# PSUM banks by step in the opening of a fused linear-attention and mixture-of-experts kernel, and norms in two halves

## The chip, the cores and the metric

One core of one Trainium2 chip. The metric is the device time of one execution in microseconds (us). A profile is one traced execution; its span is some 1.7 to 2.2 us shorter than the reported time of the same execution, so spans are compared with spans and times with times.

## The reference

Linear attention (no softmax over positions) feeds four dense experts whose outputs are added with normalised weights (condensed):

```python
def phi(x): return np.where(x > 0, x, np.exp(x) - 1.0) + 1.0
q_p, k_p = phi(q), phi(k)                       # 8 batches, 8 heads, 576 positions, 64 per head
kv  = np.einsum('bhsd,bhse->bhde', k_p, v)
num = np.einsum('bhsd,bhde->bhse', q_p, kv)
den = np.einsum('bhsd,bhd->bhs', q_p, np.sum(k_p, axis=2))[..., None] + 1e-06
x   = num / den                                 # -> 4608 rows of 512
p   = domain_probs / (domain_probs.sum(-1, keepdims=True) + 1e-09)
for e in range(4):
    out += p[:, e:e+1] * (np.maximum(x @ w1[e], 0) @ w2[e])    # 512 -> 1024 -> 512
```

## The kernel before

The kernel has an opening (0 to 27 us), in which batch 0 goes through attention as four *head pairs* while weights stream in; a first part (27 to 80 us), in which the experts run on batches 0 and 1 as plain matmuls; and the *unit* stage (80 us to the end), which is the bulk. The change touches the opening. There each pair takes these steps, on the engine named:

phi of k and q (ACT the exponential, DVE the rest); k-v sums (PE), copied out as `kvz` (ACT); transposed q (PE), copied as `qT` (ACT); products and denominators (PE); reciprocal and multiplication, the *norm* (DVE); transposed x (PE), copied (ACT). When all four pairs are there, the first layer of expert 0 can finish.

In PSUM the kernel keeps eight tiles of 512 columns, called banks here: `l1b[0..2]`, `l2b[0..3]` and `at`. A scheduler inside the kernel orders the operations, each with an engine, an estimated time, a priority and the keys it reads and writes; the framework then guards each PSUM tile as a whole (in the trace before, steps on disjoint columns of `l2b[2]` wait for each other, 5.1 us in six rows of the wait list). The part that decides who shares a bank:

```python
    def first_attention(pr, pri, step):
        ni = pr % 2
        num = (at, l2b[1])[ni]                                  # products
        kv3 = l2b[2][:, 0 : 2 * DE].rearrange(...)              # k-v sums        \
        d0 = 136 + ni * 2 * C
        den = l2b[2][:, d0 : d0 + 2 * C].rearrange(...)         # denominators     > one bank
        xt = l2b[2].bitcast(FP16)[:, NT : 2 * NT]               # transposed x    /
        # ...
        def nd(cs):
            for c in cs:                                        # two matmuls a chunk
                nc.tensor.matmul(out=num[:, c * P : (c + 1) * P], lhsT=qT[:, c],
                                 rhs=kvz[:, :, 0:D], start=True, stop=True)
                nc.tensor.matmul(out=den[:, c], lhsT=qT[:, c],
                                 rhs=kvz[:, :, D:DE], start=True, stop=True)
        # ...
        parts = 2 if pr == DC - 1 else 1                        # last pair in halves
        # ... one entry per step and half, for example:
            add("DVE", 0.93, pri + 5.5 * step, u, lambda cs=cs: norm(cs),
                r=(("num", ni), ("l2b2n", ni)), w=(("xk", pr),))
```

The leftover rows of batch 0 (64 positions beside the 512) are normalised in two groups through the bank `at` in the middle of the first part:

```python
    def rest_late(pri):
        # ...
        for p0, n in ((0, 3), (3, 1)):
            def mm(...):   nc.tensor.matmul(out=slot[pr - p0], ...)   # slot lies in `at`
            def norm(...): ...                                        # DVE, reads `at`
```

And where the scheduler expects PE to be idle early on, throw-away matmuls are put in, meant to keep its clock up ("fillers", `keep_warm()`). In the trace of the kernel before, fillers of 256 columns start 0.21 us apart until 7.6 us and, where they follow each other, 0.11 us apart after it; the granted clock is recorded there as 1.00 from 7.66 to 492.35 us.

Of the kernel before, what the change touches and what calls it, by code (L numbers as in the profile page):

```python
# [10 lines left out]
FP32 = mybir.dt.float32  # L11
FP16 = mybir.dt.float16
AO = mybir.AluOpType
AF = mybir.ActivationFunctionType
# [123 lines left out]
def kernel(  # L138
# [10 lines left out]
    nc = tc.nc  # L149

    B, H, S, D = q.shape
# [3 lines left out]
    P = 128  # L155
    NT = 512
    C = NT // P
    R = S - NT
    DE = D + 1
    DC = Dm // P  # L160
# [5 lines left out]
    WARM, COLD = 21.0, 28  # L166
# [3 lines left out]
    pl = Plan()  # L170
# [5 lines left out]
    def sb(name, shape, dt):  # L176
        return pc.tile(shape, dt, tag=name, name=name)
# [32 lines left out]
    x_b = [sb(f"x{i}", [P, C, Dm], FP16) for i in range(2)]  # L210
# [3 lines left out]
    identh = s15h[:, 0:P]  # L214
# [15 lines left out]
    v_o = [  # L230
        t[:, i * NT : (i + 1) * NT].rearrange("p (h c d) -> p h c d", h=2, c=C)
        for t in (X3[2], T3[0]) for i in range(2)
    ]
# [3 lines left out]
    v_r, kp_r = (  # L237
        T2[2][:, i * 2 * P : (i + 1) * 2 * P].rearrange("p (a b d) -> p a b d", a=2, b=2)
        for i in (2, 3)
    )  # L240
# [6 lines left out]
        A["t", 3, 1 + i] = [("kqp", 2 + i, 0), ("kqp", 2 + i, 1)]  # L247
        A["t", 2, i] = [("ek", 2 + i, 0), ("ek", 2 + i, 1)]
    A["t", 2, 2], A["w1x", 2, 0] = [("k_r", g) for g in range(DC)] + ["v_r", "kp_r"], ["ek_r"] + [("v_r32", g) for g in range(DC)]
    A["l2b1"], A["at"] = [("num", 1)], [("num", 0)]  # L250
    A["l2b3"] = [("tq", 0), ("tq", 1)]
    ones = sb("ones", [P, 2, 1], FP16)
    rc4 = sb("rc4", [P, 2, 2 * C], FP32)
    xt0 = s4_b[1].rearrange("p a c t -> p a (c t)")
    hts = [h_b[i][:, t, f].rearrange("p c t -> p (c t)") for i in range(2)
           for t in range(2) for f in range(2)]
# [16 lines left out]

    def lk(i):

        return ("l2b2k", ("l2b2n", 0), ("l2b2n", 1), "l2b2x") if i == 2 else ("l2b%d" % i,)

    def stage_keys(i):

# [196 lines left out]
    def first_attention(pr, pri, step):  # L476

        kq, sk = kqs[pr], stage_keys(pr)
        ek, kqp, vh, kvz, qT = ek_o[pr], kqp_o[pr], v_o[pr], kvs[pr], qT_b[pr % 2]
        fs = slice(pr * P, (pr + 1) * P)  # L480
        g = slice(pr * 2 * R // DC, (pr + 1) * 2 * R // DC)
        ni = pr % 2
        num = (at, l2b[1])[ni]
        tq = tbank[:, ni * NT : (ni + 1) * NT]
        kv3 = l2b[2][:, 0 : 2 * DE].rearrange("p (h e) -> p h e", h=2)
        d0 = 136 + ni * 2 * C
        den = l2b[2][:, d0 : d0 + 2 * C].rearrange("p (c h) -> p c h", h=2)
        xt = l2b[2].bitcast(FP16)[:, NT : 2 * NT]

        def phi(i, cs):  # L490
            o = kqp[:, i, cs].rearrange("p c h d -> p h c d")
            nc.vector.tensor_scalar(o, kq[:, i, :, cs], 0.0, 1.0, AO.max, AO.add)
            nc.vector.tensor_tensor(out=o, in0=ek[:, i, :, cs], in1=o, op=AO.min)

        def turn(cs):
            for c in cs:
                nc.tensor.transpose(
                    out=tq[:, c * P : (c + 1) * P], in_=kqp[:, 1, c], identity=identh
                )

        def kv():
            parts = [(kqp[:, 0, c], vh[:, :, c], ones) for c in range(C)]
            parts += [(kp_r[g, t], v_r[g, :, t], ones[g]) for t in range(2)]
            for i, (kk, vv, oo) in enumerate(parts):
                for o, x in ((kv3[:, :, 0:D], vv), (kv3[:, :, D:DE], oo)):
                    nc.tensor.matmul(out=o, lhsT=kk, rhs=x, start=(i == 0 and x is vv),  # L506
                                     stop=(i == len(parts) - 1), skip_group_check=True)

        def kvcopy():
            nc.scalar.copy(kvz[0:D, 0, :], kv3[0:D, 0, :])  # L510
            nc.scalar.copy(kvz[D:P, 1, :], kv3[D:P, 1, :])

        def nd(cs):
            for c in cs:
                nc.tensor.matmul(out=num[:, c * P : (c + 1) * P], lhsT=qT[:, c],
                                 rhs=kvz[:, :, 0:D], start=True, stop=True)
                nc.tensor.matmul(out=den[:, c], lhsT=qT[:, c],
                                 rhs=kvz[:, :, D:DE], start=True, stop=True)

        def norm(cs):  # L520
            rc = rc4[:, ni].rearrange("p (c h) -> p c h", h=2)[:, cs]
            nc.vector.reciprocal(rc, den[:, cs])
            nc.vector.tensor_tensor(  # L523
                out=x_b[0][:, cs, fs].rearrange("p c (h d) -> p c h d", h=2),
                in0=num.rearrange("p (c h d) -> p c h d", c=C, h=2)[:, cs],
                in1=rc[:, :, :, None].broadcast_to([P, cs.stop - cs.start, 2, D]),
                op=AO.mult,
            )

        def turn_x(cs):  # L530
            for c in cs:
                nc.tensor.transpose(  # L532
                    out=xt[:, c * P : (c + 1) * P], in_=x_b[0][:, c, fs], identity=identh
                )

        parts = 2 if pr == DC - 1 else 1
        m = C // parts
        halves = [(range(i * m, i * m + m), slice(i * m, i * m + m),
                   slice(i * m * P, (i * m + m) * P)) for i in range(parts)]

        def add(eng, dur, pri, u, fn, r, w):

            end = u == parts - 1
            r = tuple(r) if end else tuple((x, u) for x in r)
            w = tuple(w) if end else tuple(w) + tuple((x, u) for x in w)
            pl.add(eng, dur / parts + (0.1 if parts > 1 else 0), pri + 0.01 * u, fn, r=r, w=w)

        for i in range(2):
            pl.add("ACT", 0.62, pri + i * step, lambda i=i: nc.scalar.activation(
                ek[:, i], kq[:, i], AF.Exp), r=(sk[i],), w=(("ek", pr, i), (("ek", pr, i), 0)))  # L550
        pl.add("DVE", 0.9, pri + step, lambda: phi(0, slice(0, C)),
               r=(sk[0], ("ek", pr, 0)), w=(("kqp", pr, 0),))
        pl.add("PE", 0.5, pri + 4 * step, kv,
               r=(("kqp", pr, 0), ("v_o", pr), "v_r", "kp_r"), w=("l2b2k",))
        pl.add("ACT", 0.45, pri + 4.5 * step, kvcopy, r=("l2b2k",),
               w=(("kvz", pr), (("kvz", pr), 0)))
        for u, (cr, cs, ts) in enumerate(halves):
            add("DVE", 0.9, pri + 2 * step, u, lambda cs=cs: phi(1, cs),
                r=(("ek", pr, 1),), w=(("kqp", pr, 1),))
            add("PE", 0.24, pri + 3 * step, u, lambda cr=cr: turn(cr), r=(("kqp", pr, 1),),  # L560
                w=(("tq", ni),))
            add("ACT", 0.58, pri + 3.5 * step, u, lambda ts=ts: nc.scalar.copy(
                qT.rearrange("p c t -> p (c t)")[:, ts], tq[:, ts]), r=(("tq", ni),),
                w=(("qT", ni),))
            add("PE", 0.36, pri + 5 * step, u, lambda cr=cr: nd(cr),
                r=(("qT", ni), ("kvz", pr)), w=(("num", ni), ("l2b2n", ni)))
            add("DVE", 0.93, pri + 5.5 * step, u, lambda cs=cs: norm(cs),
                r=(("num", ni), ("l2b2n", ni)), w=(("xk", pr),))
            add("PE", 0.25, pri + 6 * step, u, lambda cr=cr: turn_x(cr), r=(("xk", pr),),
                w=("l2b2x",))  # L570
            add("ACT", 0.58, pri + 6.5 * step, u, lambda ts=ts: nc.scalar.copy(  # L571
                xt0[:, pr, ts], xt[:, ts]), r=("l2b2x",), w=(("s4", 1, pr),))

    def attention(b, pr, pe_mode, pri, step):

# [210 lines left out]
    def first_l1(e, pri, step, nb):  # L786
        ht = []
        banks = [(l1b[i], "l1b%d" % i) for i in range(3)]
        if nb > 3:
            banks[2:] = [(l2b[0], "l2b0"), (at, "at"), (l2b[3], "l2b3"), (l2b[1], "l2b1")]  # L790
            banks += [(l1b[2], "l1b2")]
        ht = [rot("ht", len(hts)) for _ in range(FC)]

# [375 lines left out]
                rest_maps(b, False, t - 2)  # L1169
            attention(b, pr, False, t, 1.5)  # L1170

    def keep_warm():

        nc.tensor.matmul(out=l1b[2][:, 256:512], lhsT=identh,  # L1174
                         rhs=qTr[0][:, 0:2].rearrange("p a t -> p (a t)"), start=True, stop=True)

    prep(0)
# [11 lines left out]
    with tc.manual_schedule(  # L1189
        engines={  # L1190
            mybir.EngineType.PE,
            mybir.EngineType.Activation,
            mybir.EngineType.DVE,
            mybir.EngineType.Pool,
            mybir.EngineType.SP,
        }
    ):
        todo = pl.order()
        free = 0.0
        warm = True  # L1200
        for o in todo:
            warm = warm and "l1b2" not in o["w"] and o["start"] < WARM
            if o["eng"] == "PE" and warm:
                gap = o["start"] - free
                for _ in range(int((gap - 0.25) / 0.115) - (COLD if free == 0.0 else 0)):
                    keep_warm()
                free = o["start"] + o["dur"]
            o["fn"]()

# [29 lines left out]
```

## Time and profile before

| before | |
|---|---|
| time, 3 runs | 497.99 us median (497.81 to 498.1) |
| profiled span | 495.8 us |
| x of batch 0 complete | 23.05 us |
| second layer of expert 0 starts | 26.60 us |
| first matmul of the unit stage | 79.66 us |

The prediction below shows the page, the waits and the timeline of the opening. In a timeline row the columns are: start (us from the start of the span), duration, engine, source line, operation, output and input names, shapes, count, and in brackets the idle time just ahead and what ended it. Matmul rows overlap at their ends (a row of 37.45 + 1.89 = 39.34, and the next from 39.18), so the pitch from one row's start to the next, divided by the count, is PE's rate.

```profile
37.45 1.89 PE L761 MATMUL l1b<-s,w 128*128 128x512 f16 x8
39.18 0.22 PE L453 MATMUL at<-s,qTr 128*128 128x130 f16 x1
```

```profile
38.41 0.55 DVE L461 TENSOR_TENSOR xr_sb<-at,rc 64x384 f16<-64x384 f32 x1
```

DVE is done with the first group in `at` at 38.96; PE writes the second group at 39.18, on its own pace (8 matmuls, 1.73 us), so 0.22 us of slack is left.

```profile
78.58 0.63 ACT L408 ACTIVATE ek<-kqr 64x512 f16<-64x512 f32 x1 [0.20 <-DMA kqr<-in_k_dram]
```

ACT waits here 0.20 us for the leftover rows of k of batch 2, and after this does copies that PE needs. A *product of the first unit* (no product of attention) is one row of eight matmuls of 128 columns on PE (L924). The first one starts at 79.66, and the third, in PE's timeline of the kernel before, at 80.93, which is 1.27 us later:

```profile
80.93 0.61 PE L924 MATMUL l1b<-xs,w1x 128*128 128x128 f16 x8
```

### The profile page before, as it was taken

The numbers are of one execution on the slowest core, as the hardware profiler recorded it, in microseconds if no ns is written. First come the engines' busy times: TensorE is split into PE (matmuls) and PEld (weight loads), VectorE is DVE, ScalarE is ACT, GpSimd is POOL, SyncE is SP. The second block draws the span as 40 slices with busy tenths as digits, with TensorE's granted clock in tenths as the row PEclk, the third lists the DMA queues.
The fourth block names the chain that finished last, engine by engine and source line by source line (L and its number), as shares of the span: only waits on it lengthen the run. The fifth ranks groups of instructions, "written<-read, shape, count | busy, mean of one in ns | idle before, by whom it ended". The sixth has DMA issues, their size and how long they took to land.

```text
span 495.8 us, 15025 instructions
## 1 busy us (share of the span) xinstructions
PE 485.8 (98%) x6108; PEld 430.3 (87%) x6108; DVE 411.5 (83%) x1041; ACT 365.2 (74%) x687; POOL 41.1 (8%) x66
## 2 busy tenths in 40 slices
PE   7899999999999999999999999999999999999995
PEld 6544557999999999999999999999999999999994
DVE  6598999999998989899988899899988676767664
ACT  5536679978977898769876997689766767676641
POOL 7656600000000000000000000000000000000000
PEclk9999999999999999999999999999999999999998
DMA  8999958956755765876556655755623333523211
GB/s 227 203 234 226 269 124 218 192 123 179 118 156 124 161 143 155 131 177 150 133 135 159 131 155 128 179 127 119 161 54 87 35 97 44 87 45 86 46 44 42
DMA packets 125541, 66.98 MB, mean 135 GB/s; under 512 B 94592, under 2 KB 119696, under 8 KB 125472
## 3 DMA queue, kind: packets, MB, share of 16 engines
q1 hardware_dynamic: 115808, 51.99, 47.5%
q0 software_dynamic: 9344, 13.71, 13.6%
q8 instruction: 47, 0.77, 0.7%
q10 hardware_dynamic: 320, 0.33, 0.2%
q14 instruction: 22, 0.18, 0.1%
HBM read 45.16 MB, written 9.44 MB: 110 GB/s over the span
## 4 chain that ended last, share of the span: by engine, by line
PE 97%; DVE 1%; ACT 1%; issue 0%; DVEq 0%
PE l1b L924 40%; PE l2b L1000 39%; PE l2b L772 6%; PE l1b L761 5%; PE at L664 2%; PE l1b L1174 2%; PE at L640 1%; PE l2b L506 0%; DVE ot L1064 0%; PE l2b L761 0%; ACT s L571 0%; PE at L643 0%; PE l2b L532 0%; DVE x L523 0%; PE l2b L616 0%
## 5 line engine op out<-in xcount | busy, mean ns | idle before, releaser
L924 PEld LDWEIGHTS <-w 128*128 128x128 f16 x2048 | 134.1, 98 | 5.4
L938 ACT ACTIVATE h<-l1b 128x512 f16<-128x512 f32 x128 | 76.6, 599 | 53.3 <-PE l1b L924 50.4
L1000 PE MATMUL l2b<-w,h 128*128 128x256 f16 x768 | 115.1, 273 | 0.0
L1000 PE MATMUL l2b<-t,s 128*128 128x256 f16 x768 | 114.6, 273 | 0.0
L924 PEld LDWEIGHTS <-w1x 128*128 128x128 f16 x1536 | 100.2, 98 | 3.8 <-issue 0.3
L1000 PEld LDWEIGHTS <-s 128*128 128x128 f16 x1024 | 90.2, 98 | 6.2
L944 DVE CUSTOM_DVE_ANT_0 h<-l1b,p 128x512 f16<-128x512 f32 x64 | 44.1, 689 | 44.0 <-PE l1b L924 41.2
L924 PE MATMUL l1b<-xT,w 128*128 128x128 f16 x1024 | 78.1, 219 | 0.0
L924 PE MATMUL l1b<-xs,w1x 128*128 128x128 f16 x1024 | 78.1, 219 | 0.0
L924 PE MATMUL l1b<-xs,w 128*128 128x128 f16 x1024 | 78.1, 219 | 0.0
L884 ACT ACTIVATE xp<-x,p_nat 128x512 f16<-128x512 f16 x112 | 77.3, 721 | 0.4
L1000 PEld LDWEIGHTS <-h 128*128 128x128 f16 x768 | 67.3, 98 | 4.5
L986 DVE TENSOR_TENSOR s<-h 128x512 f16<-128x512 f16 x128 | 53.8, 420 | 2.1
L941 ACT COPY l1b<-l1b 128x512 f32<-128x512 f32 x64 | 36.7, 574 | 12.3 <-PE l1b L924 11.7
L941 ACT COPY u<-l1b 128x512 f32<-128x512 f32 x64 | 37.4, 585 | 10.9 <-PE l1b L924 10.2
L944 DVE CUSTOM_DVE_ANT_0 h<-l1b,u 128x512 f16<-128x512 f32 x64 | 43.8, 684 | 1.7 <-PE l1b L924 0.6
L941 ACT COPY p<-l1b 128x512 f32<-128x512 f32 x64 | 37.3, 583 | 8.6 <-PE l1b L924 7.4
L902 DVE TENSOR_TENSOR xs<-xT,xs 128x256 f16<-128x256 f16 x128 | 36.8, 288 | 3.8 <-DVE xs L902 0.5
L924 PE MATMUL l1b<-xT,w1x 128*128 128x128 f16 x512 | 39.0, 219 | 0.0
L1000 PE MATMUL l2b<-w,s 128*128 128x256 f16 x256 | 38.4, 273 | 0.0
L605 ACT ACTIVATE ek<-kq 128x512 f16<-128x512 f32 x54 | 33.7, 628 | 0.1
L986 DVE TENSOR_TENSOR s<-s,h 128x512 f16<-128x512 f16 x64 | 27.2, 424 | 5.6
(155 smaller groups left out, 580.7 us busy)
## 6 DMA issues: line engine op xcount, KB each, us to landing
w<-in_moe_w_dram POOLq DMA_DIRECT2D x32, 256.0 KB, 8.0
out_dram<-ot SPq DMA_DIRECT2D x16, 512.0 KB, 3.4
kq<-in_k_dram SPq DMA_DIRECT2D x26, 256.0 KB, 3.3
kq<-in_q_dram SPq DMA_DIRECT2D x26, 256.0 KB, 3.4
vs<-in_v_dram SPq DMA_DIRECT2D x24, 256.0 KB, 3.9
xT<-xp SPq DMA_TRANSPOSE x64, 3.1
kq<-in_k_dram POOLq DMA_DIRECT2D x3, 256.0 KB, 7.1
vs<-in_v_dram POOLq DMA_DIRECT2D x3, 256.0 KB, 7.1
```

The costliest lines, as they stand in the source:

```text
L605: pl.add("ACT", 0.55, pri + i * step, lambda i=i: nc.scalar.activation(ek[:, i], kq[:, i], AF.Exp), r=(sk[i],), w=(("ek", ei, i),))
L664: nc.tensor.matmul(out=slot[c - c0], lhsT=qT[:, c] if c < C else qTr[par][:, pr], rhs=kvz, start=True, stop=True,)
L761: nc.tensor.matmul(out=bank[:, ts], lhsT=w1_sb[e][:, dc, fj * P : (fj + 1) * P], rhs=xt0[:, dc, ts], start=(dc == 0), stop=(dc == DC - 1 a ...
L772: nc.tensor.matmul(out=bank, lhsT=hts[ht[fj]][:, c * P : (c + 1) * P], rhs=w2_sb[e][:, fj, :], start=(fj == 0), stop=(fj == FC - 1),)
L884: pl.add("ACT", 0.6, pri, lambda c=c, src=src, ps=ps: nc.scalar.activation(xp[:, c, :], src, AF.Copy, scale=ps), r=r, w=(("xp", xi, c),))
L902: lambda o=o, a=a, b_=b_: tt(out=o, in0=a, in1=b_, op=AO.subtract),
L924: nc.tensor.matmul(out=bank[:, fc * P : (fc + 1) * P], lhsT=wt[:, kc, fc * P : (fc + 1) * P], rhs=r[:, kc, :], start=(start and fc == 0 an ...
L938: return lambda: nc.scalar.activation(o, bank, AF.Relu)
L941: return lambda: nc.scalar.copy(o, bank)
L944: return lambda: nc.vector._custom_dve(TENSOR_ADD_SAT, out=o, in0=bank, in1=t, s0=BIG, s1=0.0)
L986: pl.add("DVE", 0.36, U(n + 1) + d - 0.5, lambda i=i, a=a, b_=b_, alu=alu: tt(out=s4[:, i], in0=a, in1=b_, op=alu), r=r, w=(Q(i),))
L1000: nc.tensor.matmul(out=l2b[bank][:, half * HD : (half + 1) * HD], lhsT=a[:, c, :], rhs=w[:, c], start=(opens and first and c == 0), stop=( ...
```

## The change

The intent: no step of a head pair should wait for another step merely because both are in one PSUM bank. k-v sums keep `l2b[2]` alone; products and denominators go into one bank together, two chunks in `at`, two in `l2b[1]`; transposed x goes to `l1b[2]` (its last half to `l2b[3]`, by then free). Four chunks with their denominators would be 4 x 130 = 520 columns, and each of the kernel's PSUM tiles has 512, so if products and denominators are to share one, they have to be split in two: in this plan the banks and the halves come together. In return products and denominators become one matmul per chunk, and all pairs are normalised in halves, not only the last. The banks of the first layer are dealt again, and fillers get another bank.

```diff
-        num = (at, l2b[1])[ni]
-        tq = tbank[:, ni * NT : (ni + 1) * NT]
+        nds = [bank[:, 0 : C * DE].rearrange("p (c h e) -> p c h e", c=2, h=2)
+               for bank in (at, l2b[1])]
         kv3 = l2b[2][:, 0 : 2 * DE].rearrange("p (h e) -> p h e", h=2)
-        d0 = 136 + ni * 2 * C
-        den = l2b[2][:, d0 : d0 + 2 * C].rearrange("p (c h) -> p c h", h=2)
-        xt = l2b[2].bitcast(FP16)[:, NT : 2 * NT]
+        tq = tbank[:, 0:NT]
+        last = pr == DC - 1
+        xts = [l1b[2].bitcast(FP16), tbank if last else l1b[2].bitcast(FP16)]
 ...
-        def nd(cs):
-            for c in cs:
-                nc.tensor.matmul(out=num[:, c * P : (c + 1) * P], lhsT=qT[:, c],
-                                 rhs=kvz[:, :, 0:D], start=True, stop=True)
-                nc.tensor.matmul(out=den[:, c], lhsT=qT[:, c],
-                                 rhs=kvz[:, :, D:DE], start=True, stop=True)
+        def nd(u):
+            for c in range(2):
+                nc.tensor.matmul(out=nds[u][:, c], lhsT=qT[:, 2 * u + c], rhs=kvz,
+                                 start=True, stop=True)
 ...
+        for u in range(2):
+            pl.add("PE", 0.12, pri + (5 + 0.1 * u) * step, lambda u=u: nd(u),
+                   r=(("qT", ni), ("kvz", pr)), w=(("at", "l2b1")[u],))
+            pl.add("DVE", 0.63, pri + (5.5 + 0.1 * u) * step, lambda u=u: norm(u),
+                   r=(("at", "l2b1")[u],), w=(("xk", pr, u),))
+        bk = ("l1b2", "l2b3" if last else "l1b2")
 ...
-            banks[2:] = [(l2b[0], "l2b0"), (at, "at"), (l2b[3], "l2b3"), (l2b[1], "l2b1")]
+            banks[2:] = [(l2b[0], "l2b0"), (l2b[2], "l2b2"), (at, "at"), (l2b[1], "l2b1")]
             banks += [(l1b[2], "l1b2")]
 ...
-    def keep_warm():
-        nc.tensor.matmul(out=l1b[2][:, 256:512], lhsT=identh, ...
+    def keep_warm(bank):
+        nc.tensor.matmul(out=bank[:, 256:512], lhsT=identh, ...
```

## The prediction

> **What bounds the kernel now.** I read the page first (busy shares, slices, the chain that ended last), then the waits of the first 30 us, then that stretch's timeline engine by engine, since the change touches the opening alone. The page:
>
> ```profile
> PE 485.8 (98%) x6108; PEld 430.3 (87%) x6108; DVE 411.5 (83%) x1041; ACT 365.2 (74%) x687; POOL 41.1 (8%) x66
> ...
> PE   7899999999999999999999999999999999999995
> ...
> PE 97%; DVE 1%; ACT 1%; issue 0%; DVEq 0%
> ```
>
> PE sets the end. In the timeline 8 matmuls of 128 columns take 0.45 us (56 ns each), 8 of 512 take 1.73 (216 ns): from 26.6 us to about 490 it streams with no listed idle. So time can be won only before 26.6 us, where PE waits or does filler ("l1b L1174", throw-away matmuls against a cold PE). One row per reader, what it waited for, total, count, longest, for 0 to 30 us:
>
> ```profile
> DVE rc L522 <- PE l2b L506: 1.7, 2, 0.9
> ...
> PE l2b L517 <- ACT s L571: 1.0, 2, 0.6
> ...
> ACT kvz L510 <- DVE rc L522: 0.8, 1, 0.8
> ...
> DVE rc L522 <- ACT s L571: 0.7, 1, 0.7
> ...
> ACT s L510 <- PE l2b L532: 0.6, 1, 0.6
> ...
> PE l2b L506 <- DVE rc L522: 0.3, 1, 0.3
> ```
>
> None of these rows is a data dependence. The reciprocal (L522) needs the denominators (L517), not the next pair's k-v products (L506); the denominators do not need the previous pair's copy of x (L571). All live in one bank, l2b[2]: kv sums, two pairs' denominators, transposed x. Sum 5.1 us, over three engines, so partly parallel. How the waits line up at the last pair (PE's timeline, then ACT's):
>
> ```profile
> 19.28 0.40 PE L532 MATMUL l2b<-s,x 128*128 128x128 f16 x4 [0.22 <-DVE x L523]
> ...
> 20.50 0.17 PE L517 MATMUL l2b<-s,qT 128*128 128x2 f16 x1 [0.60 <-ACT s L571]
> ...
> 22.91 0.70 PE L761 MATMUL l2b<-s,w 128*128 128x512 f16 x3
> ...
> 26.60 3.62 PE L772 MATMUL l2b<-w,h 128*128 128x512 f16 x16
> ```
>
> ```profile
> 19.86 0.59 ACT L571 COPY s<-l2b 128x512 f16<-128x512 f16 x1 [0.50 <-PE l2b L517]
> 21.95 0.37 ACT L571 COPY s<-l2b 128x256 f16<-128x256 f16 x1 [1.50 <-PE l2b L532]
> 22.68 0.37 ACT L571 COPY s<-l2b 128x256 f16<-128x256 f16 x1 [0.36 <-PE l2b L532]
> ```
>
> The last half of x lands at 22.68+0.37 = 23.05. Of the first layer of expert 0 (32 matmuls x 0.216 = 6.9 us) half is then still to do: 26.6-23.05 = 3.55 us. At 26.6 the second layer starts.
>
> Last, POOL's issues, which show when weights land. From the eighteenth load on, issue n seems to wait for transfer n-8: the issue at 26.30 waited for kqr, which had been issued exactly eight loads earlier. So the starts of the waiting issues date the landings:
>
> ```profile
> 19.84 1.06 POOL L292 DMA_DIRECT2D w<-in_moe_w_dram  x2 [0.75 <-DMA w<-in_moe_w_dram]
> ...
> 26.30 0.72 POOL L292 DMA_DIRECT2D w<-in_moe_w_dram  x1 [0.41 <-DMA kqr<-in_q_dram]
> ...
> 46.16 0.72 POOL L292 DMA_DIRECT2D xp<-in_k_dram  x1 [0.54 <-DMA w<-in_moe_w_dram]
> ```
>
> By this count the last quarter of expert 0's w1 lands at 19.8, its w2 at 21.1 to 25.1, expert 1's w1 by 30.7, expert 2's w1 at 46.1.
>
> [...]every wait above is between disjoint columns of one bank. [...] Here the first fillers take 5.26/24 = 219 ns, later ones 1.25/10 = 125; no gap after 8 us reaches 1 us[...].
>
> **The change, part by part.**
>
> Removed: the shared bank. kv keeps l2b[2] alone; products go with their denominators, two chunks each, into `at` and l2b[1]; transposed x goes to l1b[2], the last half to l2b[3]. PE also saves: 4 x (128-column + 2-column) at 0.08 us a couple = 0.34 us a pair become 4 matmuls of 130 columns at about 0.055 = 0.22 us; four pairs, 0.5 us.
>
> Added: norms in halves for all pairs. Measured half: reciprocal start 20.86 to next start 21.41 = 0.55 us; two = 1.1, against 0.24+0.61 = 0.85 for a whole one. Three pairs x 0.25 = 0.75 us of DVE, which idles over 5 us between 9 and 24. The last pair loses its halves in phi, transpose and qT: about 0.4+0.2+0.2 = 0.8 us of latency.
>
> Moved: first-layer banks. `at` and l2b[1] now stay taken until the last norm, l1b[2] until the last pair's first x copy; l2b[2] takes l2b[3]'s place.
>
> The new opening by hand, from measured durations, each step at the later of its data and its engine. Data are unchanged: they come by DMA, k of pair 3 about 13.0 (issued 7.87, 5.1 to landing), q 13.7 (8.58+5.1), v 14.9. Up to the second phi of pair 1 (ends 11.23) all is as before.
> DVE, the busiest engine here: norm 0 (products at 10.8 to 11.2, no longer behind pair 1's kv) 11.2 to 12.3; phi of pair 2, q (0.95 a phi) to 13.2; norm 1 13.4 to 14.5, its products waiting for qT (copied 12.4 to 13.0 after kvcopy); the two phi of pair 3 14.5 to 16.3; norm 2 16.3 to 17.4, its products long ready.
> Pair 3 on PE and ACT: transposes of q end 16.8 (0.41 after phi), qT 17.45 (0.59), first products 17.75; DVE norm 3 17.8 to 18.95 in halves; first half of x transposed 18.45 to 18.7 and copied 18.8 to 19.15; second half transposed by 19.3, copied by 19.7.
> So x is complete about 19.7 in the ideal order, say 20.5 in the real one, instead of 23.05.
>
> PE then: with four banks usable early, two quarters of the contraction (8 matmuls) fit before 18.6, when quarter three's weights (18.5) and x of pair 2 (about 18.5) are there. Left: 24 x 0.216 = 5.2 us and 0.2 of transposes, so the first layer ends at 24.0. This is PE-bound; x has some 1.5 us to spare. Before: 26.6 to 26.8. Ideal gain 2.7 us. I take off 0.5 for in-order holes (the old opening has such ones at 18.9, 19.9 and 21.4) and 0.2 for what follows downstream: **2.0 us**. After the opening PE's work is unchanged, so the end moves by the same amount: 498.0-2.0 = **496.0 us**.
>
> **Rivals.**
>
> *Weights take the place of the wait.* With L1 of expert 1 at 33.5-2.0 = 31.5 its weights (by 30.7) are there, with 0.8 us to spare; that of expert 2 starts at 48.8-2.0 = 46.8 against 46.1. DMA was over full share from 10 to 60 us, so loads cannot come earlier. It speaks for this that a gain over 2.7 us would touch the landing; against it, that a gain of 2 does not. If it binds: 496.5 to 497.
>
> *DVE becomes the bound.* DVE is nearly gapless from 62 to 92 us (18.9 of 20 us busy in 80 to 100) and sits at 91% in 100 to 200. Moving PE earlier moves its deadlines. But DVE's own start, the first relu at 23.76, moves too, and around 74 to 78 it does work due much later (weight sums of the last expert, phi of batch 2). If it binds, half the gain goes: 497.
>
> *The new banks bring new waits.* Three banks are locked later than before, and fillers now write l2b[2], where kvcopy reads, so a filler can hold PE until a copy is done. For it: the remainder after x is bigger, 3.5 to 4.3 us. Against: PE has work in other banks meanwhile. If the order came out badly: 498 to 499.
>
> *All goes to plan:* 495.2.
>
> **Range and chances.** The size of the shift is what I doubt, not its direction. 8 in 10: 495.1 to 497.4. 2% is 10 us, more than all idle PE time before 26.6; so faster by over 2% 0.01, within 2% 0.98, slower 0.01.
>
> **What would show each step.** Right: the six wait rows gone or under 0.3 us; the last x copy done at 20 to 21; the second layer starting at 24.2 to 25.2 without PE idle after it; the unit stage (first L924) at 77.2 to 78, not 79.7; the gap in the start of the second layer equal to the gap in the span. Wrong: PE waiting for a DMA or for DVE between 26 and 100 us; x late because norms queue on DVE; holes of PE over 0.5 us between 17 and 24; fillers waiting for ACT on l2b[2]; matmuls of twice the duration, a lost clock.

Some passages are cut, and the cuts marked. The forecast: 2.7 - 0.5 - 0.2 = 2.0 us. The DMA that it calls "over full share" has shares of 1.07 to 1.19 in the trace from 10 to 60 us, taken in stretches of 2 to 8 us; that loads could not come earlier for this reason is the author's estimate.

## The result

| | before | after |
|---|---|---|
| time, median (range), 4 runs each | 497.9 us (497.51 to 498.1) | 496.46 us (496.36 to 497.32) |
| ratio | | 0.9976 [0.9959, 0.9993] |
| profiled span | 495.8 us | 494.7 us |
| x of batch 0 complete | 23.05 | 20.69 |
| second layer of expert 0 starts | 26.60 | 24.67 |
| first matmul of the unit stage | 79.66 | 77.98 |
| fifth product of the first unit | 81.82 | 80.61 |
| from there to the end of the span | 414.0 | 414.1 |

Ratios here and below are the mean time of one kernel's runs over that of the kernel before in the same rounds, so not quite the ratio of the medians; the brackets are 95% intervals. Every run gave correct results. The change gains about 0.2%, well inside the 2% within which a time counts as the same.

The page of the kernel after, busy shares and the chain that ended last:

```profile
PE 484.2 (98%) x6092; PEld 429.3 (87%) x6092; DVE 413.0 (83%) x1045; ACT 364.8 (74%) x686; POOL 41.0 (8%) x66
...
PE 91%; DVE 3%; DMA 3%; ACT 1%; POOL 1%; issue 1%; DVEq 0%; SPq 0%; ACTq 0%
```

PE has 16 matmuls fewer (four pairs of four chunks, each with one matmul where there were two), DVE four operations more and 1.5 us more of work. The chain is the telling line: before it was PE to 97%, now DMA and DVE have 3% each.

The waits of all engines from 0 to 30 us, of the kernel after; columns: engine, what it was about to write, line, releaser, total, times, longest:

```profile
PEld L528 <- DVE x L519: 1.3, 3, 0.7
...
DVE rc L518 <- PE at L513: 1.1, 1, 1.1
...
PE at L513 <- ACT kvz L509: 0.9, 1, 0.9
```

The six false waits of before (5.1 us) are gone. What is left follows the data: x is transposed after its norm, the reciprocal waits for its own denominators, the products for `kvz`. PE's timeline of the kernel after shows what bounds the opening now:

```profile
14.48 0.22 PE L504 MATMUL l2b<-t 128*128 128x128 f16 x1 [0.59 <-DMA t<-in_v_dram]
...
19.25 0.38 PE L750 MATMUL l1b<-s,w 128*128 128x512 f16 x1 [0.45 <-ACT s L533]
...
23.59 1.25 PE L750 MATMUL l1b<-s,w 128*128 128x256 f16 x6
24.67 1.67 PE L761 MATMUL l2b<-w,h 128*128 128x512 f16 x7
```

First, PE waits at 14.48 for v of pair 2, which is a load: in the profiled executions of the kernels below that share this opening this start lies anywhere from 14.08 to 15.60 us. Second, from 19.25 PE runs without a listed wait to the second layer. The last copies of x, ACT of the kernel after:

```profile
19.77 0.37 ACT L533 COPY s<-l1b 128x256 f16<-128x256 f16 x1 [0.57 <-PE l1b L528]
20.32 0.37 ACT L533 COPY s<-l2b 128x256 f16<-128x256 f16 x1 [0.17 <-PE l2b L528]
```

x is complete at 20.32 + 0.37 = 20.69, four microseconds before the first layer ends.

So the opening gives 26.60 - 24.67 = 1.93 us, but the span only 1.1. From the fifth product of the first unit to the end both kernels take 414 us, so the 0.83 us are lost between 24.67 and 80.61. The same milestones, as differences, localise it: from the second layer of expert 0 to the first layer of expert 1 both take 6.90; from there to expert 1's second layer 7.46 before and 7.72 after (0.26 lost); from there to the first unit matmul 38.70 and 38.69; from there to the fifth product 2.16 and 2.63 (0.47 lost); and 0.11 over the remaining 414 us.

**First loss, at 37.5 us.** PE's timeline and then DVE's of the kernel after:

```profile
35.56 1.89 PE L750 MATMUL l1b<-s,w 128*128 128x512 f16 x8
37.51 0.22 PE L451 MATMUL at<-s,qTr 128*128 128x130 f16 x1
```

```profile
36.91 0.55 DVE L459 TENSOR_TENSOR xr_sb<-at,rc 64x384 f16<-64x384 f32 x1
```

The eight matmuls now take 1.95 us to the next row instead of 1.73, and the next row begins just after DVE has read `at` (36.91 + 0.55 = 37.46). No wait is listed, since gaps this short do not reach the list; the pitch shows it. PE had come 1.89 us earlier to this place (37.45 to 35.56), DVE only 1.50 (38.41 to 36.91), and the slack was 0.22: 1.89 - 1.50 - 0.22 = 0.17, near the 0.22 us that were lost in this pitch. DVE started 2.47 us earlier (its first relu at 21.29 instead of 23.76) and works back to back from there, but between this relu and the first scaling of the second layer's rows it does nine weight sums instead of eight, each 0.6 us. That is most of the 0.97 us by which it came less early to the norm.

**Second loss, at 79.7 us.** ACT's and then PE's timeline of the kernel after:

```profile
75.38 1.33 ACT L873 ACTIVATE xp<-x,p_nat 128x512 f16<-128x512 f16 x2
78.04 0.63 ACT L406 ACTIVATE ek<-kqr 64x512 f16<-64x512 f32 x1 [1.33 <-DMA kqr<-in_k_dram]
```

```profile
79.72 0.61 PE L913 MATMUL l1b<-xs,w1x 128*128 128x128 f16 x8 [0.20 <-ACT l1b L930]
```

The load of k's leftover rows, issued at 73.56, lands only at 78.04, 4.5 us later; before it took 3.3. ACT waits 1.33 us for it, the copy that PE needs next stands behind this exponential in ACT's order and is late, and PE waits: its third product starts 79.72 - 77.98 = 1.74 us after the first, instead of 1.27. This is the whole 0.47.

Why the load takes 1.2 us longer is the question that took most of the experiments. One more view, the DMA queues in half a microsecond: the kernel before from 73.0 to 73.5,

```profile
q8 instruction: 1, 0.02, 12.3%
```

and the kernel after from 75.0 to 75.5:

```profile
q1 hardware_dynamic: 170, 0.04, 37.1%
q8 instruction: 1, 0.02, 12.0%
```

(Columns: queue and kind, packets, MB, share of the 16 DMA engines.) Queue q8, of the kind that the profile calls `instruction`, has 47 packets of 16 KB in the whole execution, here called *blocks*. PE has 6,108 matmuls and as many weight loads, 12,216 instructions, so 260 a block. In the packed trace of the kernel before the first block starts when 255 of PE's recorded instructions have begun and the last at 11,946, on average 254 apart (after: 253, 11,978 and 255). So the blocks seem to go with the count of PE's instructions. Before, the block at 73.3 us came when no other queue moved anything, ahead of the transfers for the unit stage. In the kernel after PE has 32 instructions fewer ahead of this point (16 matmuls, 16 weight loads), so by its count the block comes 16 x 0.216 = 3.5 us later against the work, an estimate from PE's measured rate, and it falls among these transfers. In the two traces it comes 6.3 us ahead of the first unit matmul before, and 2.7 after. This is a theory at this place; its test is the last group of experiments.

### The profile page after: what moved, and what is told of

Read it like the earlier page. It is cut to its first block, busy times and chain, and to the rows that moved or that the text cites. A ratio compares the mean times of both kernels' runs of the same rounds, so it can differ in the third digit from the quotient of the medians. Undisturbed runs are those within 1.5% of the kernel's fastest.

```text
span 494.7 us, 14994 instructions
## 1 busy us (share of the span) xinstructions
PE 484.2 (98%) x6092; PEld 429.3 (87%) x6092; DVE 413.0 (83%) x1045; ACT 364.8 (74%) x686; POOL 41.0 (8%) x66
## 4 chain that ended last, share of the span: by engine, by line
PE 91%; DVE 3%; DMA 3%; ACT 1%; POOL 1%; issue 1%; DVEq 0%; SPq 0%; ACTq 0%
PE l1b L913 40%; PE l2b L989 39%; PE l1b L750 4%; PE l2b L761 3%; PE at L653 2%; PE at L629 1%; DMA t<-in_v_dram 1%; DMA kqr<-in_k_dram 1%; DVE t L736 1%; DMA kq<-in_k_dram 1%; POOL w1x L290 1%; DVE w1x L715 1%; DVE ot L826 1%; PE l2b L750 0%; DVE ot L1053 0%
## 5 line engine op out<-in xcount | busy, mean ns | idle before, releaser
L930 ACT COPY l1b<-l1b 128x512 f32<-128x512 f32 x64 | 36.8, 574 | 12.0 <-PE l1b L913 11.4
```

Source lines behind the costliest of these rows:

```text
L930: return lambda: nc.scalar.copy(o, bank)
```

## The experiments

Twelve kernels ran, four at a time on one chip, each four beside runs of the kernel before. One execution of each was traced. In five of the twelve (banks alone, halves with one key, PE delayed, the changed kernel with loads early, the kernel before with 32 instructions fewer) it was the slowest of its kernel, so the spans of these five are above what their other executions show. Below, *opening* is the time from the k-v sums of pair 2 to the second layer of expert 0, which takes the luck of v's landing out; it is 11.90 in the kernel before and 10.19 after.

### The change again

Edit: none.

> The changed kernel once more, as the control of this set. Span of the profiled run 494.7 us within 0.3, about 1.2 us under the kernel before; second layer of expert 0 starts at 24.7, unit stage (first L913) at 78.0. What I look at: the load of the rest rows of k for batch 2, which took 4.5 us to land in the first look and 3.3 before. Theory 'the late landing belongs to the new timing': 4 us or more again, PE idle some 0.45 us around 79.5, end at 494.7. Rival 'chance of one run': 3.3 us, no idle there, span 494.2.

Measured: 496.71 us (496.35 to 497.08), ratio 0.9975 [0.9963, 0.9988]; span 494.6, opening 10.19. The loss at 37.5 us was 0.09 (7.55 against 7.46), that at the unit stage 0.94 (3.10 against 2.16). PE's wait list from 24 to 84 us of this run has one row:

```profile
PE at L632 <- DVE kqpr L402: 0.6, 1, 0.6
```

The gain is reproduced. The loss at the unit stage shows again, and larger, with another engine at the end of the same chain (ACT's exponential is late, so DVE's part of phi is).

### Which part gives the gain: banks alone

To the kernel before: denominators to `l2b[0]`, transposed x to `l1b[2]`, norms whole as they were.

```diff
-        den = l2b[2][:, d0 : d0 + 2 * C].rearrange("p (c h) -> p c h", h=2)
-        xt = l2b[2].bitcast(FP16)[:, NT : 2 * NT]
+        den = l2b[0][:, d0 : d0 + 2 * C].rearrange("p (c h) -> p c h", h=2)
+        xt = l1b[2].bitcast(FP16)
```

(The banks of the first layer and of the fillers are dealt anew.)

> The other part alone: whole products and norms as before (halves for the last pair only), but denominators, k-v sums and transposed x in three different banks. Theory 'the shared bank was the cost': second layer of expert 0 starts at 24.7 to 25.4, span 494.7 to 495.0. Rival 'halves count': 26 or later, span 495.4 or more.

Measured: 497.5 us, ratio 0.9993 [0.998, 1.0007], span 496.4. The opening took 10.57, and the second layer started at 24.87: 1.73 us earlier than before. Nothing of it reached the end: 1.67 us were lost between the two layers of expert 1 (9.13 against 7.46), and 0.6 more after the fifth product, which no listed wait explains. PE's and then ACT's timeline of this run:

```profile
38.46 1.02 PE L762 MATMUL l1b<-s,w 128*128 128x512 f16 x4 [0.38 <-ACT h L800]
40.05 1.02 PE L762 MATMUL l1b<-s,w 128*128 128x512 f16 x4 [0.57 <-ACT h L800]
```

```profile
37.29 0.63 ACT L606 ACTIVATE ek<-kq 128x512 f16<-128x512 f32 x1 [1.79 <-DMA kq<-in_k_dram]
...
38.88 0.63 ACT L603 CAST vp<-vs 128x512 f16<-128x512 f32 x1 [0.47 <-DMA vs<-in_v_dram]
```

ACT stood 1.79 us waiting for k of batch 1, which had not come earlier with the rest, and the relus behind it in ACT's order kept PE waiting. The opening's gain is mostly a matter of banks (1.33 of 1.71 us, with two matmuls a chunk and whole norms as before); whether it survives depends on what stands ahead of the relus in ACT's order 13 us later. In the changed kernel the order happens to be kinder; this is not a merit of the halves that any run shows.

### Which part gives the gain: halves, with k-v sums and x in one bank

To the kernel after: transposed x back to `l2b[2]`, first with one scheduler key for the bank.

```diff
-        xts = [l1b[2].bitcast(FP16), tbank if last else l1b[2].bitcast(FP16)]
+        xts = [l2b[2].bitcast(FP16)[:, NT : 2 * NT]] * 2
-        bk = ("l1b2", "l2b3" if last else "l1b2")
+        bk = ("l2b2", "l2b2")
```

(Here too the banks of the first layer and of the fillers change.)

> Products and norms in halves with their denominators, as in the changed kernel, but k-v sums and the transposed x share one bank (l2b[2]), as they did before. Theory 'the shared bank between the steps of neighbouring pairs was the cost': most of the gain of the opening is lost, second layer of expert 0 starts at 25.6 to 26.4 (before 26.60, after 24.67), span 495.2 to 495.8. Rival 'the halves and the denominators beside their products are what counts': start at 24.6 to 25.2, span 494.7.

Measured: 504.05 us, ratio 1.0121 [1.0106, 1.0137], clock 0.987. This run does not answer its question. The single key made the scheduler finish one pair's x before the next pair's sums, and the last fillers start at 12.9 us; PE then lost its clock. PE's timeline of this run, and the row of the granted clock in 40 slices from the page:

```profile
15.56 0.38 PE L750 MATMUL l1b<-s,w 128*128 128x512 f16 x1
18.96 1.04 PE L750 MATMUL l1b<-s,w 128*128 128x512 f16 x2
```

```profile
PEclk9789999999999999999999999999999999999998
```

A matmul of 512 columns had a pitch of 0.22 us at 15 us and of 0.43 at 19 to 28 us; the trace has a granted clock of 1.00 until 18.86 us and 0.50 after it. PE was not idle before the drop: from 15.45 to 18.86 us its matmuls are listed as busy for 2.07 us. So in this run the clock fell while PE had work; what brings it down is not shown.

So once more, with two keys for the bank, as the kernel before had:

```diff
+        return ("l2b2k", "l2b2x") if i == 2 else ("l2b%d" % i,)
-        bk = ("l1b2", "l2b3" if last else "l1b2")
+        bk = ("l2b2x", "l2b2x")
```

(Cut: the edit of `xts` above, the other keys, the banks of the first layer and of the fillers.)

> The halves with shared bank once more, now with k-v sums and transposed x as separate entries of the scheduler, as they were in the kernel before, so that it may interleave the pairs although they share l2b[2] (in the first try the one entry forced an order pair after pair, and PE lost its clock). Theory 'the shared bank was the cost': second layer of expert 0 starts at 25.4 to 26.6, later than with banks of their own (24.3 to 24.9). Rival 'the halves are enough': 24.3 to 25.0.

Measured: span 495.0, second layer at 24.39, opening 10.20, the same as with the full change: the theory failed and the rival held. The last copy of x, ACT of this run:

```profile
20.90 0.37 ACT L533 COPY s<-l2b 128x256 f16<-128x256 f16 x1 [0.60 <-PE l2b L528]
```

x is complete at 21.27, 0.6 us later than in the kernel after although v landed 0.3 us earlier, and it costs nothing: PE is the bound. A bank of its own for transposed x is therefore not needed; getting the denominators out of the bank of the k-v sums is what both this kernel and "banks alone" share. Moving the denominators and nothing else was not run. The time is another matter: 497.65 us (497.15 to 499.47), ratio 1.0003 [0.9985, 1.0022], with 0.51 us lost between 38.75 and 77.96 and 0.76 at the unit stage.

### Where the rest went: is PE simply too early?

Four throw-away matmuls of 512 columns (0.86 us) between the two layers of expert 0, in the kernel after. If both losses come from PE's being early, they should shrink by that.

```diff
+                for _ in range(4):
+                    nc.tensor.matmul(out=l2b[3], lhsT=identh, rhs=w1_sb[0][:, 0, 0:512],
+                                     start=True, stop=True)
```

> The changed kernel with four throw-away matmuls of 512 columns (4 x 0.216 = 0.86 us of PE) just ahead of the second layer of expert 0, nothing else, the order of all other instructions the same. It gives 0.86 of the 1.93 us won in the opening back. Theory 'what was lost later is lost to things that keep their time, weights landing at 30.7 and 35.3 and the loads of batch 2': the waits of PE at 37.5 (0.25) and at 79.5 (0.47) shrink, the span grows by only 0.2 to 0.5 us, to 494.9 to 495.2. Rival 'the waits are in the new order of instructions': they stay, span 494.7+0.86 = 495.5.

Measured: 497.32 us, ratio 0.9991 [0.9978, 1.0004], span 496.5; v of pair 2 landed 1.1 us later than in the kernel after, so PE was 1.98 us later at the second layer in all. The loss at 37.5 us was gone (7.46). The loss at the unit stage was not (2.65 from first matmul to fifth product), and its wait stood elsewhere; ACT of this run:

```profile
78.39 1.33 ACT L874 ACTIVATE xp<-x,p_nat 128x512 f16<-128x512 f16 x2 [1.28 <-DMA xT<-xp]
```

Here the transposing DMA (`xT`) took 4.4 us instead of 3.1, the load of k's rows 4.2. With PE back at before's times the transfers were as slow as in the kernel after. So the first loss is a matter of PE's being early against DVE, the second is not. (In the halves with two keys, whose order of work differs, PE came to the place at 37.5 us still earlier and lost nothing there, so it is the distance to DVE that counts.) The span fits neither expectation: it is above both, with v late and in the slowest execution of the five.

### Where the rest went: a bank for the second group of leftover rows

The second group goes to `l2b[3]`, so PE need not wait for DVE's norm of the first.

```diff
+            dst = at if p0 == 0 else l2b[3]
-                        out=slot[pr - p0], lhsT=qTr[0][:, pr], rhs=kvs[pr], start=True, stop=True
+                        out=dst[:, (pr - p0) * 2 * DE : (pr - p0 + 1) * 2 * DE],
+                        lhsT=qTr[0][:, pr], rhs=kvs[pr], start=True, stop=True
```

> The changed kernel with the second group of products of batch 0's rest rows (one matmul and its norm at about 37.5 us) in l2b[3], free at that time, instead of in the bank of the first group. Orders are the same. Theory 'PE waits there for DVE's norm of the first group, DVE being late because it waited for weights at 30.3 and 35.1': the PE wait of 0.25 us at 37.5 goes, unit stage starts at 77.7 instead of 78.0. In the span it shows only if the loads of batch 2 do not eat it: 494.45 to 494.7. Rival: PE waits elsewhere instead, unit stage at 78.0.

Measured: the loss is gone, 7.49 instead of 7.72; PE of this run:

```profile
35.70 1.89 PE L752 MATMUL l1b<-s,w 128*128 128x512 f16 x8
37.42 0.22 PE L452 MATMUL l2b<-s,qTr 128*128 128x130 f16 x1
```

The pitch is 1.72 again, although DVE reads the first group until 37.59 in this run, later than PE writes the second. The same edit gives 1.72 in its two combinations below; without it the repeat had 1.83, and the kernel with 32 instructions more 1.95. So the wait was for the bank, and for DVE behind it. The time did not follow: 497.47 us, ratio 0.999 [0.9978, 1.0002], span 495.2, because the unit stage lost 1.07 (3.23).

### Where the rest went: the leftover rows of batch 2 loaded earlier

Theory at this point: the loads of the leftover rows are issued too late for the earlier PE. They are moved ahead in SP's order, in the kernel after, in the kernel before, and in the kernel after together with the bank above.

```diff
+        moved = [o for o in todo if o.get("early")]
+        todo = [o for o in todo if not o.get("early")]
+        i = max(i for i, o in enumerate(todo) if o.get("ahead")) + 1
+        todo[i:i] = moved
```

> The changed kernel with one move: the three loads of the rest rows of batch 2 are issued on SP right after the loads of its first pair, before the first transposing DMA instead of after it (some 5 us earlier). All other orders are the same. Theory 'ACT waits for these loads in front of the copy that PE needs at 79.5': that wait of 1.3 us goes, the PE idle of 0.47 us at 79 to 80 goes, span 494.7-0.47 = 494.2. Rival 'PE is held there by something else (DVE, the transposed x)': no change in the span, 494.7.

> The same move in the kernel before, as a control. There ACT waited 0.2+0.2 us for these loads and PE had no idle listed. Theory: span 495.8, at most 0.2 less. Rival 'the late loads cost the kernel before as much': 495.3.

> Both moves together. If the two losses are the whole difference between the gain of the opening (1.93 us) and that of the span (1.1): span 495.8-1.9 = 493.9 to 494.1, 1.7 to 1.9 us under the kernel before. If a later bound takes it: 494.5 or more.

| | time | ratio | span | first unit matmul to fifth product |
|---|---|---|---|---|
| after, loads early | 496.88 | 0.9984 [0.9967, 1.0002] | 497.7 | 3.83 |
| before, loads early | 497.86 | 1.0003 [0.9991, 1.0015] | 496.1 | 2.16 |
| after, loads early and bank | 496.98 | 0.9983 [0.9971, 0.9996] | 495.8 | 3.59 |

The theory fell. The loads were issued 2.7 to 6.8 us earlier, and the wait moved to the next transfer; ACT of the kernel after with early loads:

```profile
79.89 1.33 ACT L875 ACTIVATE xp<-x,p_nat 128x512 f16<-128x512 f16 x2 [2.68 <-DMA xT<-xp]
```

The transposing DMA now took 5.8 us. (The profiled execution of this kernel was its slowest, 499.51 us; the others took 495.93 to 497.23, so its span is not typical.) In the kernel before the same edit did no harm and no good. So it is not the place of a certain load: in all kernels so far derived from the changed one some transfer between 72 and 80 us is slow, and in the kernel before none. That led to the instruction blocks.

### What makes the transfers slow: shifting PE's instruction count by 32

In the kernel after 16 fillers of 256 columns are split into two of 128: 32 more instructions with the weight loads, the same columns. In the kernel before 32 fillers are merged two by two into 16: 32 fewer. No other operation is touched. If the instruction block is the cause, the first should behave like the kernel before at the unit stage, and the second like the kernel after.

```diff
 # kernel after
+        if len(split) < 16:
+            split.append(1)
+            for i in range(2):
+                nc.tensor.matmul(out=bank[:, 256 + i * P : 256 + (i + 1) * P], lhsT=identh,
+                                 rhs=qTr[0][:, i], start=True, stop=True)
+            return
```

```diff
 # kernel before
+                    if n > 1 and len(merged) < 16:
+                        merged.append(1)
+                        nc.tensor.matmul(out=l1b[2], lhsT=identh,
+                                         rhs=qTr[0].rearrange("p a t -> p (a t)"), start=True, stop=True)
+                        n -= 2
+                        continue
```

(A *packet* is a block of queue q8, the *rows* are PE's instructions.)

> The changed kernel with 16 of its throw-away matmuls of 256 columns at the start written as two of 128 columns each: the same PE time, but 32 more rows in PE's program (12218, as the kernel before has; the change has 12186). All other instructions and orders are the same. Theory '[...]32 rows fewer moved one such packet from 73.0 us, where the DMA stood idle, to 74.5 to 75 us, into the transposed x and the rest rows of batch 2, and these then came about 1 us late': the packet is back at about 71, these loads take 3.1 to 3.5 us instead of 4 to 5, from unit 0's first matmul to its fifth product 2.1 to 2.3 us pass instead of 2.63 and 3.10, span 493.8 to 494.3. Rival 'the new timing or order delays them': 2.6 or more as before, span 494.6.

> The opposite in the kernel before: 32 of its throw-away matmuls of 256 columns written as 16 of 512, so that PE's program has 12186 rows, at the same PE time. Theory of the program fetch: the packet comes 3.5 us later, at about 76.5, among the same transfers, which take 4 us or more; from unit 0's first matmul to its fifth product 2.5 to 3.1 us instead of 2.16; span 496.2 to 496.8 (495.8 before). Rival: nothing moves, 2.16 and 495.8.

And the first together with the bank for the second group of leftover rows:

> The best version that the runs point to: the changed kernel with the 32 rows and with the second group of rest products in its own bank. If both losses are gone: from the start of expert 0's second layer to unit 0 53.06 to 53.1 us, to the fifth product 2.2, then 414.0 to the end, so span 24.6+53.1+2.2+414.0 = 493.9, 1.9 us under the kernel before (ratio 0.9962). If something later takes it: 494.5.

| | time | ratio | span |
|---|---|---|---|
| after, 32 instructions more | 496.46 (496.06 to 497.12) | 0.9975 [0.9962, 0.9987] | 494.5 |
| before, 32 fewer | 497.75 (497.56 to 498.77) | 1.0003 [0.999, 1.0015] | 496.9 |
| after, 32 more, and bank | 496.84 (496.03 to 497.3) | 0.9978 [0.9964, 0.9992] | 495.3 |

ACT of the kernel after with 32 more, then ACT and PE of the kernel before with 32 fewer:

```profile
77.10 0.63 ACT L406 ACTIVATE ek<-kqr 64x512 f16<-64x512 f32 x1 [0.15 <-DMA kqr<-in_k_dram]
```

```profile
79.14 1.33 ACT L884 ACTIVATE xp<-x,p_nat 128x512 f16<-128x512 f16 x2 [1.99 <-DMA xT<-xp]
```

```profile
81.72 0.23 PE L643 MATMUL at<-vpr,kqpr 128*128 128x130 f16 x1 [0.67 <-DVE kqpr L404]
```

The wait of 1.33 us shrinks to 0.15 in the one, and the other, which is the kernel before but for 32 fillers made into 16, gets a wait of 1.99 us and then one of PE. All runs together, with the time at which the block of instructions appears (in steps of 0.25 us), the issue of the first transposing DMA of the unit stage, and the times from issue to landing of it and of k's leftover rows:

| kernel | block at | `xT` issued | `xT` took | k rows took | first unit matmul to fifth product |
|---|---|---|---|---|---|
| before | 73.25 | 73.82 | 3.1 | 3.3 | 2.16 |
| banks alone | 72.5 | 72.03 | 3.8 | 3.1 | 2.21 |
| after, 32 more | 72.0 | 72.38 | 3.1 | 3.1 | 2.25 |
| after, 32 more, bank | 72.75 | 73.15 | 3.1 | 3.2 | 2.25 |
| before, loads early | 73.75 | 74.17 | 3.1 | (earlier) | 2.16 |
| after | 75.25 | 72.14 | 3.2 | 4.5 | 2.63 |
| after, again | 74.5 | 71.58 | 5.1 | 4.2 | 3.10 |
| after, PE delayed | 75.0 | 73.87 | 4.4 | 4.2 | 2.65 |
| after, bank | 75.0 | 72.06 | 5.2 | 4.1 | 3.23 |
| halves, two keys | 74.25 | 72.34 | 4.7 | 4.2 | 2.92 |
| before, 32 fewer | 76.75 | 73.92 | 5.1 | 4.0 | 3.17 |

Where the block comes ahead of the transposing DMA or within half a microsecond of its issue, transfers take 3.1 to 3.8 us and the stage starts in 2.16 to 2.25. Where it comes 1 to 3.1 us after that issue, one or both transfers take 4.0 to 5.2 us and the stage takes 2.63 to 3.23. Shifting it by 32 instructions moves a kernel from one group to the other, in both directions. That the block goes with PE's program can be counted in the packed traces: in all fourteen this packet starts when PE has begun 923 to 937 matmuls and weight loads (929 before, 931 after), wherever that falls in time. This I call shown, for the profiled executions, one of each kernel. (Not in the table are the two kernels derived from the changed one with early loads, and the one that lost its clock; their blocks came 3.2 to 3.5 and 2.4 us after the issue, and their stages took 3.59, 3.83 and 2.92.)

Two things stay open. The size: the block takes 12% of 16 engines for 0.5 us, so about 1.0 us of one engine. If a transfer had to wait for all of that, it would land about 1 us later, an estimate from this number. Measured are 0.7 to 2.1. In what way a block delays a transfer, and the rest of the delay, no run shows. And the times. The profiled span of the kernel with 32 instructions more (494.5; expected 493.8 to 494.3) is only 0.2 us under that of the kernel after, since its second layer started 0.21 us later; its ratio is the same 0.9975. The kernel before with 32 fewer is no slower in its times than the kernel before, though its span is 1.1 us longer: the traced execution was the slowest of five, and the other four have spans of 495.6 to 496.0, where the kernel before in the same rounds has 495.3 to 496.4. The intervals are 0.6 us to either side, so half a microsecond cannot be seen in them, but the 1.0 us that this stage lost in the trace would show. So the block explains the traces; that it costs as much in ordinary executions is not shown.

The last kernel, with both losses mended, should have been the best and was not: its span is 495.3. Both mends work in it (pitch 1.72 at the leftover rows, and 2.25), but v of pairs 2 and 3 landed late (opening 10.74), and DVE waited 0.83 us at 47.5 for a weight load of expert 2, which cost PE another 0.5 us. None of the twelve beats the change by more than its interval.

## Why the prediction was right, and where it was wrong

The time was predicted as 496.0 us and measured as 496.46, inside the range of 495.1 to 497.4, and within 2%, as it had been given 98 in 100. The gain was forecast as 2.0 us and measured as 1.2 by the ratio (1.4 by the medians): the mechanism in the opening was right, and what follows was worth more than was taken off for it.

- *The bound.* Right: six false waits of 5.1 us, none left. The opening was worth 1.93 us in the profiles (1.71 with the landing of v taken out), against 2.2 in the prediction before its deduction for what follows.
- *The opening by hand.* DVE came within 0.2 us of it through the second pair's norm and phi of pair 3 (norm 0 predicted at 11.2 to 12.3, measured 11.4 to 12.5; norm 2 16.3 to 17.4, measured 16.4 to 17.5). It slipped at pair 3, whose products came at 18.4 instead of 17.75, since other matmuls stood ahead in PE's order. PE, too, came close: 8 matmuls of the first layer ran early, as predicted, and the other 24 started at 19.25 instead of 18.6, when pair 2's copy of x was done, and took the 5.4 us predicted. x was complete at 20.69, predicted "20.5 in the real one".
- *PE-bound afterwards, x with time to spare.* Right, and shown by the halves with a shared bank: x 0.6 us later, the same start of the second layer.
- *Halves cost DVE, pitch 0.55.* Right: 18.73 to 19.29 for two reciprocals, 1.5 us more DVE work on the page.
- *"0.2 for what follows downstream".* This is the term that was mis-sized: it was 0.83 us. The prediction's check, the same gap in the second layer and in the span, failed (1.93 and 1.1). In its place the runs showed two things. 0.26 us (0.09 in the repeat) is the second rival, set aside too fast: DVE's start did move by 2.5 us, but of this only 1.5 was left at the leftover rows' norm, mostly for one more weight sum in its order, and PE waits for the bank there. 0.47 us (0.94 in the repeat) was in no rival: in the traced executions a block of the instruction queue falls among the transfers of the unit stage.
- *First rival, weights.* Not binding for PE at 31.6 and 47.1 us in the changed kernel; the estimated 46.1 for expert 2's weights was near enough to the edge that one variant met it (0.83 us of DVE at 47.5).
- *Third rival, new waits.* Not seen: no filler waits for ACT in the list, and PE's one hole of note between 17 and 24 us is the 0.45 us at 19.25, for a copy of x that its matmul reads.
- *What the prediction missed in the opening.* Removing the false waits put v of pair 2 on the critical path (0.59 us of PE at 14.5). In the kernel before, PE was not at that point early enough to see when v landed; now it is. That this makes the times less steady is not shown: the changed kernel's own nine runs lie within 496.35 to 497.32 us, those of the kernel before within 497.23 to 498.83.

## What to carry to other kernels

When steps share a PSUM bank, look for waits between engines with no data between them: here giving the denominators a bank with their products removed six of them (5.1 us) for the price of a few more DVE operations (four, 1.5 us). Of the 1.93 us won in the early stage 1.1 reached the end of the span; most of the rest was lost where the earlier PE met a bank that DVE still read (0.26 us) and late transfers (0.47). So follow the earlier engine to each place where it meets loads, or an engine with work of its own, and find the slack there (here 0.22 us at one place). And when a change of some instructions in one place goes with slower transfers elsewhere in the trace, see where the blocks of the instruction queue fall before a cause is sought in the data: here a block that came 1 to 3.1 us after a transposing DMA's issue went with one or two landings of 4.0 to 5.2 us instead of 3.1 to 3.8.
